# An H3 long convolution and an MLP on one core: unit (1,0)'s spectra without sums, last rows of y kept on chip, later matrix splits, and Strassen's scheme for one more block

## The chip, the cores and the metric

The kernel runs on one core of one Trainium2 chip. The time is the device time of one execution in microseconds. Before the change three timed runs took 859.74, 860.5 and 862.29 us, with a median of 860.5 us. The engines are TensorE (PE, with its weight loads shown as PEld), VectorE (DVE), ScalarE (ACT), GpSimd (POOL) and SyncE (SP); here SP issues nearly all DMA transfers. Each engine takes its instructions in the order in which the program gives them.

## The reference

Sequence length S is 2048, width D is 640, the MLP's inner width is 1728, all in float32. Cut to what matters:

```
x = A_q
for layer in range(2):
    x = x + A(layernorm(x), k, v, shift_k, ssm_k, ssm_D)
    x = x + relu(layernorm(x) @ w1) @ w2

def A(q, k, v, shift_k, ssm_k, ssm_D):
    kv = causal_conv4(k, shift_k) * v          # per channel
    y  = causal_conv_2048(kv, ssm_k)           # per channel, by FFT of length 4096
    return q * (y + kv * ssm_D)
```

`y` doesn't depend on `x`, so both layers use the same `y`, which the kernel computes once.

## The kernel before

The sequence is cut into 8 chunks of 256 rows (each two half chunks `s` of 128 rows), the width into 5 tiles of 128 channels.

*The convolution.* The work is done in units: one chunk and two channel tiles, or two chunks and one tile, or a single tile. Unit (c,t) is named by its first chunk and tile. `transform` computes for a unit the 256-point spectra of its `kv` (tile `at`) and of its piece of the filter (tile `gt`), both on TensorE with float32 matrices of cosines and sines (`cM`, `cG`, `cX`). For the filter, two sources `hf` and `hr` (the filter's chunk and the reversed chunk before it) are first added and subtracted on VectorE (`gs`, L415); TensorE multiplies these with four matrices, one bank per parity (`pg`, L470); ScalarE copies the odd bank (`ob`, L474), and VectorE forms sum and difference (`gt`, L475 and L476). For chunk 0, where only `hf` exists, the program multiplies `hf` directly with matrices and their negatives (L447), two banks, and ScalarE copies the banks to `gt` (L450). `products` multiplies spectra of chunk pairs on VectorE (768 columns in three parts, L592 to L596), adds them up, transforms back on TensorE (`pq`, L618 or L327 to L329) and writes the two half chunks of `y` to a tile `ys` (L650 and L651), which is stored to DRAM (L659). The spectra of chunks 0 to 5 also go out to DRAM (L540, L541) and are loaded again for later chunks. From the seventh unit on, the forward transform of `kv` uses `cM` as a pair of high and low parts (`csplit`, L319 to L323, whose results are `cMh` and `cMl`); later units use such a pair of `cG` as well.

*The weights.* `norms` loads `w1` and `w2` in 28 tiles (`ws`, L691), sums their squares on TensorE (`pw`, L698; the diagonal is taken by `dg`, L703; summed over partitions with a matrix of ones, `pn`, L705) and makes a power of two of each norm (`wsc`, L709). `wsplit` then splits each tile into a high and a low float16 part, on ScalarE (L725) and VectorE (L726), in an order in which the tiles of `w2` follow those of `w1` by WLAG = 3 groups.

*The MLP.* `main` runs once per block: (chunk, layer, half chunks). The first two chunks are done in halves, 8 short blocks; the other six chunks in whole blocks, 12 of them, in the order (2,0), (3,0), (2,1), (3,1), (4,0), (5,0), (4,1), (5,1), (6,0), (7,0), (6,1), (7,1), where the second number is the layer. A block goes through 7 groups `j` of 256 inner columns in the order JS = 0, 1, 2, 3, 6, 4, 5: the first product (`h`, L1024 to L1027, three passes of float16), the relu split into two float16 parts (`hh`, `hl`), and the second product (`o` and `oc`, L996 to L999), which runs one group behind. For a block in the list WINO the second product is done by Strassen's scheme with 7 products in place of 8 (L951), in six PSUM banks. It needs sums of `w2`'s quarters, which `wcombine` computes: DMA of `w2` again, four VectorE operations (`wc`, L755 to L758), a scaled copy on ScalarE (L766) and its low part on VectorE (`wt`, L767), one group after the other, and only after the last convolution product has written `gate`. Some groups of such a block stay plain, in the Strassen banks: group 6 always, and for a block of layer 0 before chunk 7 the first EARLY groups of JS too. `prep` forms a block's input: it loads `y` from DRAM (L842), takes the layer norm, multiplies by `y` (L845), adds, and normalizes again.

*The order of the work.* Nothing runs in the order of the program's text. Each operation is put into a list with its engine, a cost, what it reads and writes and a priority; `Plan.order` goes through time by these costs and gives each engine, when it is free, the ready operation of the best priority. The names are CRIT = -1, URGENT = 0, SOON = 1, CONV = 2, LATER = 2.5 and FILL = 3 (the MLP's matmuls are FILL), with the place in the program as the tie-break. It models DMA as one stream of a given bandwidth (DBW0 and DBW), and a buffer of a ring (`T(pool, tag, count, ...)`) must be free before an operation that first writes it can start. What comes out is the order on each engine's queue; on the chip an engine waits where its next instruction isn't ready. The loads of a unit have the unit's priority, and the weights' have SOON.

## Time and profile before

| | |
|---|---|
| median of three timed runs | 860.5 us |
| the profiled execution | 861.58 us |
| its span, first to last instruction | 859.8 us |
| PE, PEld busy | 842.6, 661.3 us |
| DVE, ACT, POOL busy | 743.3, 481.9, 46.5 us |
| mean granted clock of TensorE | 0.996 |
| DMA moved | 178.04 MB, mean 207 GB/s |

The profile shows one execution on the chip. A row of the order in time gives the start in us, the length in us, the engine, the source line, the operation, output and inputs by the program's tile names, their shape and type and a count of merged instructions; in square brackets stands the idle time of the engine before the row and what ended it. A row of the costliest groups gives the count, then busy us and mean ns, then idle us. Rows of DMA issues give the size and the median time from issue to landing. Matmuls are pipelined and their ends are modelled, so the starts of consecutive ones give their rate. "SPq" is SP's queue issuing a transfer.

### The profile page before, as it was taken

To read this page: it belongs to the slowest core of one execution; us is meant where nothing else is said; L and a number is where in the kernel's file an instruction comes from. 1 tells how busy PE (TensorE), PEld (TensorE's weight loads), DVE (VectorE), ACT (ScalarE), POOL (GpSimd) and SP (SyncE) were. 2 spreads that over 40 slices of the span, in tenths; PEclk is the share of its full clock that TensorE was granted. 3 is DMA by queue.
4 is the path that set the end of the run, shared out by engine and by line. 5 is a ranking of instruction groups with operands and counts; after the bars stand their busy time and mean duration, and the time that the engine had idled before them with its cause. 6 is when DMAs were issued, how large, how long until landed. Compare 5 with 4: busy or idle time off the path is not lost.

```text
span 859.8 us, 19550 instructions
## 1 busy us (share of the span) xinstructions
PE 842.6 (98%) x7738; PEld 661.3 (77%) x7738; DVE 743.3 (86%) x1367; ACT 481.9 (56%) x1121; POOL 46.5 (5%) x57
## 2 busy tenths in 40 slices
PE   8899999999999999999999999999999999999997
PEld 7777878777878777777777777778777777888886
DVE  6999999999889999999999998999897576645543
ACT  6597486455686375728448383745416275727331
POOL 2000000000011001101010000000000000000000
PEclk9999999999999999999999999999999999999999
DMA  9994868798999979889698879687985371110200
GB/s 325 389 295 136 261 197 295 213 344 280 312 249 294 315 205 260 214 247 249 199 245 245 225 230 167 177 192 237 260 285 200 109 240 32 41 23 1 42 21 32
DMA packets 133837, 178.04 MB, mean 207 GB/s; under 512 B 50545, under 2 KB 87153, under 8 KB 133746
## 3 DMA queue, kind: packets, MB, share of 16 engines
q1 hardware_dynamic: 125426, 166.31, 61.9%
q0 software_dynamic: 8320, 10.49, 8.3%
q8 instruction: 60, 0.98, 0.5%
q14 instruction: 31, 0.25, 0.1%
HBM read 122.03 MB, written 34.08 MB: 182 GB/s over the span
## 4 chain that ended last, share of the span: by engine, by line
PE 76%; DVE 14%; DMA 5%; ACT 2%; issue 2%; SPq 1%; DVEq 0%; ACTq 0%
PE h L1024 11%; PE h L1027 11%; PE h L1025 11%; PE o L997 7%; PE o L996 7%; PE o L999 7%; PE o L951 7%; DMA ws<-in_w 3%; DVE pd L595 3%; DVE pacc L596 3%; PE oc L996 2%; PE oc L997 2%; PE oc L999 2%; PE pq L618 1%; PE hb L1024 1%
## 5 line engine op out<-in xcount | busy, mean ns | idle before, releaser
L1027 PE MATMUL h<-xT,w 128*128 128x256 f16 (+1 forms) x1290 | 301.6, 252 | 0.4 <-DVE w L726 0.4
L1024 PE MATMUL h<-xT,w 128*128 128x256 f16 (+1 forms) x1290 | 301.9, 252 | 0.0
L1025 PE MATMUL h<-xT,w 128*128 128x256 f16 (+1 forms) x1290 | 301.7, 252 | 0.0
L1024 PEld LDWEIGHTS <-w 128*128 128x128 f16 x1390 | 136.1, 98 | 10.6 <-ACT w L731 0.4
L1025 PEld LDWEIGHTS <-w 128*128 128x128 f16 x1390 | 136.2, 98 | 10.3
L997 PE MATMUL o<-w,hh 128*128 128x512 f16 x364 | 137.9, 379 | 0.4 <-DVE w L726 0.4
L996 PE MATMUL o<-w,hh 128*128 128x512 f16 x364 | 138.1, 380 | 0.0
L1027 PEld LDWEIGHTS <-w 128*128 128x128 f16 x1290 | 126.4, 98 | 9.6 <-DVE w L726 0.6
L596 DVE TENSOR_TENSOR pacc<-pacc,pd 128x768 f32<-128x768 f32 x140 | 133.0, 951 | 0.5
L1080 ACT ACTIVATE hh<-h 128x512 f16<-128x512 f32 (+1 forms) x103 | 50.4, 489 | 102.1 <-PE h L1027 98.2
L997 PEld LDWEIGHTS <-hh 128*128 128x128 f16 x728 | 71.2, 98 | 45.7
L996 PEld LDWEIGHTS <-hh 128*128 128x128 f16 x728 | 71.2, 98 | 44.5 <-issue 0.2
L999 PE MATMUL o<-w,hl 128*128 128x512 f16 x234 | 88.7, 379 | 0.6 <-DVE hl L1081 0.6
L997 PE MATMUL oc<-w,hh 128*128 128x128 f16 x364 | 79.7, 219 | 0.0
L996 PE MATMUL oc<-w,hh 128*128 128x128 f16 x364 | 79.7, 219 | 0.0
L595 DVE TENSOR_TENSOR pd<-Ax,Gx 128x768 f32<-128x768 f32 x83 | 77.9, 951 | 0.7 <-DMA Gx<-G 0.5
L999 PEld LDWEIGHTS <-hl 128*128 128x128 f16 x468 | 45.8, 98 | 28.6 <-DVE hl L1081 1.1
L999 PE MATMUL oc<-w,hl 128*128 128x128 f16 x234 | 51.2, 219 | 0.0
L393 ACT ACTIVATE tp<-kt,shs 128x256 f32<-128x256 f32 (+1 forms) x78 | 42.7, 574 | 14.8 <-DVE acc L430 10.7
L1081 DVE SCALAR_TENSOR_TENSOR hl<-h,hh 128x512 f16<-128x512 f32 x55 | 37.7, 685 | 8.2 <-ACT hh L1080 8.2
L595 DVE TENSOR_TENSOR pd<-at,Gx 128x768 f32<-128x768 f32 x46 | 43.2, 952 | 1.7 <-DMA Gx<-G 1.6
L411 POOL DMA_DIRECT2D gs<-hr x20 | 19.6, 980 | 387.5 <-DVE pacc L592 189.5
(230 smaller groups left out, 1662.9 us busy)
## 6 DMA issues: line engine op xcount, KB each, us to landing
Ax<-A SPq DMA_DIRECT2D x89, 384.0 KB, 4.6
Gx<-G SPq DMA_DIRECT2D x89, 384.0 KB, 4.1
G<-gt SPq DMA_DIRECT2D x30, 384.0 KB, 4.9
A<-at SPq DMA_DIRECT2D x30, 384.0 KB, 4.4
y<-Y SPq DMA_DIRECT2D x30, 320.0 KB, 4.7
ws<-in_w SPq DMA_DIRECT2D x28, 320.0 KB, 6.6
x<-in_q SPq DMA_DIRECT2D x16, 320.0 KB, 4.6
out_dram<-x SPq DMA_DIRECT2D x16, 320.0 KB, 3.6
```

The costliest lines, as they stand in the source:

```text
L393: ACT.activation(o[:, i : i + m], kview(i, m, j), AF.Copy, scale=shs[:, t, j : j + 1])
L595: ew(f"mac{j % POOLMOD}", 768, lambda e, pd=pd, av=av, gv=gv: e.tensor_mul(pd.t, av(), gv()), [ax, gx], [pd], pr_)
L596: dve(768, lambda i=i, pd=pd: DVE.tensor_add(acc[:, i], acc[:, i], pd.t), [acc, pd], [acc], pr_)
L951: PE.matmul(b[:, c : c + w], x, y[:, z : z + w], start=done[i] == 1, stop=done[i] == total[i])
L996: PE.matmul(z, hh[:, c], wh[:, d], start=(j == JS[0] and i == 0 and (h == 0 or s == S[0])), stop=False)
L997: PE.matmul(z, hh[:, c], wl[:, d], start=False, stop=end and tail)
L999: PE.matmul(z, hl[:, c], wh[:, d], start=False, stop=end)
L1024: PE.matmul(p[:, z], wh, xv(t, 0), start=b, stop=False)
L1025: PE.matmul(p[:, z], wh, xv(t, 1), start=False, stop=tail and e)
L1027: PE.matmul(p[:, z], wl, xv(t, 0), start=False, stop=e)
L1080: act(2 * R, lambda p=p, hh=hh: ACT.activation(hh.t, p.t, AF.Relu), [p], [hh], URGENT)
L1081: dve(2 * R, lambda p=p, hh=hh, hl=hl: DVE.scalar_tensor_tensor(hl.t, p.t, 0.0, hh.t, op0=ALU.max, op1=ALU.subtract), [p, hh], [hl], URGENT)
```

## The change

1. `STRAIGHT` = ((1, 0),): unit (1,0)'s filter spectra are formed from `hf` and `hr` directly, as chunk 0's are from `hf`: 16 matmuls in place of 4, no `gs`, no `ob`, no `gt` sums on VectorE; ScalarE copies two banks. `cX` gets a third matrix (the negative of one of `cG`). Its `hf` and `hr` are loaded with priority SOON + 0.02, and the tiles of `w2` get SOON + 0.04, so these two loads stand between `w1` and `w2`.
2. `STRAIGHT_Y` = (1, 2, 4, 6): for these chunks, in layer 0, `prep` loads only those columns of `y` that were stored before the last unit of the chunk (a marker `YW` stands for their stores), and multiplies the last columns straight from that unit's `ys`, which stays in its buffer until then. All of `y` is still stored, for layer 1.
3. `ones` is a constant of its own and no longer takes one of the two `u` buffers.
4. The split of `cM` moves behind `wsplit` in the program, with the second split tile of `w2` group `JS[3]` as an added dependence.
5. `WINO` gets (6, 0), and `EARLY` is 2 and not 3. (6,0) is the only block to which EARLY applies: its groups 2, 3, 4 and 5 use Strassen's scheme, 0, 1 and 6 stay plain. All of the convolution and `wcombine` now stand in the program before the `prep` of (6,0) and not of (7,0).
6. The planner's `WLAG` is 4 and not 3, and its DMA model gets two stalls, 1.9 us at 3.5 and 1.3 us at 15.
7. `SIGNED` is a way to transform products back without the sum and difference on VectorE. It is empty, so none of its code runs; but its two matrices `cN` are loaded.

```diff
-WLAG = 3
+WLAG = 4
+STALLS = ((3.5, 1.9), (15.0, 1.3))
+SIGNED = ()
+CMJ = 3
+STRAIGHT_Y = (1, 2, 4, 6)
+STRAIGHT = ((1, 0),)
-WINO = ((7, 0), (6, 1), (7, 1))
-EARLY = 3
+WINO = ((6, 0), (7, 0), (6, 1), (7, 1))
+EARLY = 2
...
+                while best.nbytes and stalls and now >= stalls[0][0]:
+                    dma = max(dma, now + DLAT) + stalls.pop(0)[1]
...
+        straight = u[0] in STRAIGHT
...
-            dma(4 * n * wd, lambda x=x, src=src: SP.dma_start(x.t, pieces(u, src)), [], [x], LP.get(u[0], pr_))
+            dma(4 * n * wd, lambda x=x, src=src: SP.dma_start(x.t, pieces(u, src)), [], [x], SOON + 0.02 if straight and k[0] == "h" else LP.get(u[0], pr_))
...
-            if c0:
+            if c0 or straight:
                 gs.append((hf, lambda: hv(hf)))
                 continue
...
-        if c0:
+        if c0 or straight:
+            srcs = [hf] if c0 else [hf, hr]
             for b in range(2):
                 for ri in range(2):
+                    for k, x in enumerate(srcs):
...
+                        def f(b=b, ri=ri, k=k, x=x):
+                            for eo in range(2):
+                                neg = (b and eo) ^ (ri and k)
+                                m = cXt[:, ri if eo else 2, :] if neg else cGt[:, 2 * eo + ri, :]
+                                PE.matmul(e4(pg[b])[:, :, ri, :], m, hv(x)[:, eo], start=ri + eo + k == 0, stop=ri + eo + k == 1 + len(srcs))
...
+                        pe(8 * mm4, f, [x, cGt] + [cXt] * (b or ri and k), [pg[b]], pr_)
                 act(w, lambda b=b: ACT.activation(gt[:, :, 0:2, b, :], e4(pg[b]), AF.Copy), [pg[b]], [gt], pr_)
...
+                    early_w = c_ in STRAIGHT_Y and u[-1][1] < NDT - 1
...
+            for a in {c_ for c_, _ in u if u[-1][1] == NDT - 1 and c_ in STRAIGHT_Y}:
+                LASTY[a] = (ys, [t for c_, t in u if c_ == a][0], [i for i, (c_, _) in enumerate(u) if c_ == a])
...
-        ones = T(cv, "u", 2, [P, P], "ones", stream=1)
+        ones = keep(const, [P, P], "ones")
...
-                    dma(4 * D, lambda t=t, src=src: SP.dma_start(t.t, src), [], [t], SOON)
+                    dma(4 * D, lambda t=t, src=src: SP.dma_start(t.t, src), [], [t], SOON + 0.04 * k)
...
+            near = LASTY.pop(a, None) if layer == 0 else None
+            cut = near[1] * P if near else D
...
-                dma(4 * D, lambda s=s: SP.dma_start(ys[s].t, Y_d[s][a].t), [Y_d[s][a]], [ys[s]], SOON)
+                dma(4 * cut, lambda s=s: SP.dma_start(ys[s][:, 0:cut], Y_d[s][a].t[:, 0:cut]), [YW[a, s] if near else Y_d[s][a]], [ys[s]], SOON)
...
+                ew("ay", cut, lambda e, s=s, xn=xns[s]: e.tensor_mul(xn[:, 0:cut], ys[s][:, 0:cut], xn[:, 0:cut]), [ys[s], xns[s]], [xns[s]], URGENT)
+                if near:
+                    yt, k = near[0], near[2]
+                    ew("ay", D - cut, lambda e, s=s, xn=xns[s], yt=yt, k=k: e.tensor_mul(xn[:, cut:D], yt[:, s, k[0] : k[-1] + 1, :].rearrange("p a b -> p (a b)"), xn[:, cut:D]), [yt, xns[s]], [xns[s]], URGENT)
...
-    cXt = cload(cG[:, 4:6], "X", 2, CP[1], T(cv, "ru", NRU, [P, 2, P], "cX", stream=1))
+    cXt = cload(cG[:, 4:7], "X", 3, CP[1], T(cv, "ru", NRU, [P, 3, P], "cX", stream=1))
     cMt = cload(cM, "M", 6, CP[2])
+    cNt = cload(cG[:, 7:9], "N", 2, CP[2], T(cv, "ru", NRU, [P, 2, P], "cN", stream=1))
...
-    cMs = csplit(cMt, 6)
     conv_to(0)
...
     wsplit()
     xT = xTs[0]
+    cMs = csplit(cMt, 6, False, [WT[JS[CMJ], 1, 1]])
```

More of the change, by code (lines that the diff above doesn't have):

```diff
@@ L157, in when @@
             return max([now, *(when(d, depth - 1) for d in o.deps)]) + o.cost + 0.08
-        finish, later = [], []
+        finish, later, stalls = [], [], list(STALLS)
         now = 0.0
@@ L600, in products @@
         direct = u[-1][0] == 0
+        signed = direct and u[0] in SIGNED
         us = []
@@ L613, in products, with g @@
             fv = lambda f=f: f.r("p a (b c) -> p a b c", b=2)
+            if signed:
+                for s in range(2):
+                    def g(ri=ri, s=s, fv=fv):
+                        for kk in range(2):
+                            m = cNt[:, kk, :] if ri and not s else cMt[:, ri + 4 * kk, :]
+                            PE.matmul(pq[:, s * 256 : s * 256 + h], m, fv()[:, :, kk, :], start=ri + s + kk == 0, stop=ri + s + kk == 3)
+                    pe(8 * mm4, g, [f, cMt] + [cNt] * (ri and not s), [pq], pr_ if ri <= s or not s else BACK)
+                continue
             if full:
@@ L646, in products @@
             yo = lambda s: ys[:, s]
-        qs = T(cv, "qs", 1, [P, n, P], "qs" + nm)
-        act(h, lambda: ACT.activation(qs.t, pq[:, 256 : 256 + h].rearrange("p (a b) -> p a b", a=n), AF.Copy), [pq], [qs], pr_)
+        yq = lambda s: pq[:, s * 256 : s * 256 + h].rearrange("p (a b) -> p a b", a=n)
+        if signed:
+            for s in range(2):
+                act(h, lambda s=s: ACT.activation(yo(s), yq(s), AF.Copy), [pq], [dst[s]], (SOON, URGENT)[s])
+        qs = T(cv, "qs", 1, [P, n, P], "qs" + nm) if not signed else None
+        if not signed:
+            act(h, lambda: ACT.activation(qs.t, pq[:, 256 : 256 + h].rearrange("p (a b) -> p a b", a=n), AF.Copy), [pq], [qs], pr_)
         pp = lambda: pq[:, 0:h].rearrange("p (a b) -> p a b", a=n)
-        dve(h, lambda: DVE.tensor_sub(yo(0), pp(), qs.t), [pq, qs], [dst[0]], pr_)
-        dve(h, lambda: DVE.tensor_add(yo(1), pp(), qs.t), [pq, qs], [dst[1]] + [gate] * (u is units[-1]), BACK if direct else pr_)
+        if not signed:
+            dve(h, lambda: DVE.tensor_sub(yo(0), pp(), qs.t), [pq, qs], [dst[0]], pr_)
+            dve(h, lambda: DVE.tensor_add(yo(1), pp(), qs.t), [pq, qs], [dst[1]] + [gate] * (u is units[-1]), BACK if direct else pr_)
         if direct:
```

17 lines of the change are left out of this document (8 added, 9 removed).

## The prediction

> **What bounds the kernel now.** I read the page first: the busy shares, the 40 slices, the chain.
>
> ```profile
> span 859.8 us, 19550 instructions
> PE 842.6 (98%) x7738; PEld 661.3 (77%) x7738; DVE 743.3 (86%) x1367; ACT 481.9 (56%) x1121; POOL 46.5 (5%) x57
> ...
> DVE  6999999999889999999999998999897576645543
> ...
> PE 76%; DVE 14%; DMA 5%; ACT 2%; issue 2%; SPq 1%; DVEq 0%; ACTq 0%
> ```
>
> TensorE has matmuls in flight for 842.6 of 859.8 us, so at most 17.2 us are waits; the rest moves only if matmul work goes away or runs at a higher clock. VectorE is nearly as full until slice 30 (645 us) and has room after it. The profiled execution took 861.58 us (span 859.8, 1.8 around it); the three timed runs have median 860.5, 1.1 less. So I look for where TensorE waits. First TensorE's instructions in order of time, before the first MLP matmul (`h`), and the table of stretches (length, then busy us of PE, PEld, DVE, ACT, POOL, the granted clock, DMA share, GB/s):
>
> ```profile
> 40.81 0.71 PE L898 MATMUL xt<-ident,xh 128*128 128x128 f16 x5 [0.62 <-ACT xh L862]
> 42.33 0.72 PE L898 MATMUL xt<-ident,xl 128*128 128x128 f16 x5 [0.80 <-DVE wpw L708]
> 42.84 0.31 PE L1012 MATMUL h<-xT,w 128*128 128x128 f16 x1
> ```
> ```profile
> 35.65:42.84 7.19, 3.92 (x38) 2.70 (x39) 5.81 (x25) 5.77 (x11) 0.00 (x0) 0.82 1.06 385
> 42.84:46.90 4.06, 4.06 (x41) 4.06 (x40) 3.67 (x10) 3.39 (x8) 0.00 (x0) 0.50 1.03 403
> 48.00:60.00 12.00, 11.09 (x133) 8.67 (x131) 11.74 (x21) 11.63 (x26) 0.00 (x0) 1.00 0.98 294
> 60.00:80.00 20.00, 19.19 (x224) 14.09 (x222) 19.83 (x42) 15.21 (x29) 0.00 (x0) 1.00 0.39 130
> ```
>
> The MLP starts at 42.84. In the 7.19 us before it TensorE is idle 3.27 us, and the first 4.06 us of the MLP run at clock 0.50, which is 2.0 us lost. From 48 to 80 us 1.7 us more are lost. All later waits of TensorE that the timeline marks with over 0.5 us are these, 2.7 us in sum:
>
> ```profile
> 169.32 0.39 PE L999 MATMUL o<-w,hh 128*128 128x512 f16 x1 [0.59 <-DVE hh L1081]
> ...
> 176.13 1.18 PE L470 MATMUL pg<-gs,cG 128*128 128x256 f32 x4 [1.48 <-ACT at L520]
> ...
> 543.38 0.39 PE L999 MATMUL o<-w,hl 128*128 128x512 f16 x1 [0.59 <-DVE hl L1081]
> ```
>
> **The change part by part.** What holds the MLP start is VectorE's queue; its rows, with the DMA queue's issues:
>
> ```profile
> 14.90 0.17 DVE L779 TENSOR_SCALAR negmA<-sumq 128x2 f32<-128x2 f32 x1 [1.39 <-ACT jq L815]
> ...
> 22.51 0.95 DVE L322 TENSOR_TENSOR cMl<-cM,cMh 128x768 fp32r<-128x768 f32 x1
> ...
> 39.46 0.29 DVE L703 SCALAR_TENSOR_TENSOR dg<-pw,ident 128x128 f32<-128x128 f32 x1 [1.38 <-PE pw L698]
> 39.67 0.16 DVE L861 RECIPROCAL rstdB<-stdB 128x1 f32<-128x1 f32 x1
> ...
> 41.39 0.88 DVE L863 SCALAR_TENSOR_TENSOR xl<-xc,rstdB,xh 128x640 f16<-128x640 f32 x1
> ...
> 49.41 0.68 DVE L415 TENSOR_TENSOR gs<-hf,hr 128x512 f32<-128x512 f32 x1
> ...
> 73.58 0.68 DVE L475 TENSOR_TENSOR gt<-pg,ob 128x512 f32<-128x512 f32 x1
> ```
> ```profile
> 13.16 19.68 SPq L691 DMA_DIRECT2D ws<-in_w  x24
> ...
> 36.51 0.37 SPq L379 DMA_DIRECT2D hf<-in_hF  x1
> 37.27 0.37 SPq L379 DMA_DIRECT2D hr<-in_hR  x1
> ```
> ```profile
> ws<-in_w SPq DMA_DIRECT2D x28, 320.0 KB, 6.6
> ```
>
> Start of the MLP. The matrices' split (`cMl`) leaves a VectorE queue that is full from 15 to 37 us: -0.9 us (its 0.95 row less the overlap with the next); it comes back after the weight split, beside matmuls, at nothing on the path while VectorE has room, else 0.9. The second norm (`dg`), which waits for the last weight tile, stands ahead of `rstdB`; without it `rstdB` would run about 0.8 us earlier (39.67 less 39.46 is its own length, the wait was 1.38, and a square root stands before it). The new order is computed with two DMA stalls (1.9 and 1.3 us) that the old one did not know, so its idea of the last weight tile moves back and `rstdB`, `xh`, `xl` should be put ahead of `dg`: -0.8. Against it stand bytes. `cX` grows by 64 KB, a new `cN` of 128 KB, which nothing reads, goes out behind `cM` and ahead of `x`, on which VectorE already waits 1.39 us at 14.90: 192 KB at 385 GB/s is up to 0.5 us, I take +0.3. The `hf` and `hr` of unit (1,0), 512 KB, move from 36.5 to between `w1` and `w2`: another 1.4 us on the last `w2` tile. That is behind the first `h`, which needs only `w1` and `x`, unless `dg` still blocks the queue. `w1` and `w2` splits lie four groups apart instead of three, which gives `w2` a later due time, and no new instructions. Sum for the start: -1.4, from -1.7 to +1.9 (last weight tile 0.5 + 1.4 = 1.9 us later and `dg` still ahead).
>
> Spectra of (1,0) straight. TensorE's rows for a chunk-0 unit, which is computed this way already (two instructions are one fp32 matmul of 256 columns), and for (1,0) now:
>
> ```profile
> 16.04 0.59 PE L447 MATMUL pg<-hf,cG 128*128 128x256 f32 x2
> 16.47 0.59 PE L447 MATMUL pg<-hf,cX 128*128 128x256 f32 x2
> ...
> 52.36 1.08 PE L470 MATMUL pg<-gs,cG 128*128 128x256 f32 x4
> ```
>
> A matmul takes 0.43 us from start to start. Straight needs 2 halves x 2 parts x 2 sources x 2 parities = 16 of them, 6.9 us, in place of 4, 1.7 us. Off VectorE go two `gs` and two `gt` of about 0.6 us each, 2.4 us; ScalarE copies two banks instead of one. The weight tiles go out every 0.82 us from 13.16 on, four before; the h data follow the 14th (21.4 us) and land 6.6 us later, near 28 to 30 us, and the matmuls rank ahead of MLP matmuls (2 against 3), and the gap of 3.27 us before 42.84 shrinks with the earlier start, so I let 2.6 us of the 6.9 disappear in it and 4.3 us fall into the MLP: +2.6 net. Bounds: all hidden, -1.7; none hidden, +5.2.
>
> The clock. That filling makes the gap dense. Up to 40 us the clock holds while TensorE has such work, and the 0.50 comes after the thin 7.19 us; I take the nearest row, dense work before 35 us, and let the MLP start warm: -2.0 (bounds -2.0 and 0). The Trainium skill, "TensorE: Matmul & The Clock Gate", section "What's actually happening", has the gate fall to half after an idle window of about 3.4 us and rise after a busy one, with a free-running window. The 4.06 us at 0.50 agree with it; by that rule a gap filled only in part may still leave the start cold, and the sum would be 2.0 us higher.
>
> The MLP's first 40 us go at the pace of the weight split, which VectorE sets:
>
> ```profile
> L726 DVE SCALAR_TENSOR_TENSOR w<-ws,wsc,w 128x640 f16<-128x640 f32 x28 | 24.0, 878 | 0.6 <-ACT w L725 0.5
> ```
>
> 24.0 of its 33 us up to 73 us are this. It gets 0.8 (wait), 0.9 (`cMl`) and 1.2 (`gs`) us of room, so of the 1.7 us lost from 48 to 80 I let half go: -0.9 (bounds -1.7 and 0).
>
> `ones` among the constants frees a second `u` buffer in the start, where VectorE is full anyway: 0. Last rows of `y`:
>
> ```profile
> y<-Y SPq DMA_DIRECT2D x30, 320.0 KB, 4.7
> ```
>
> The last columns of chunks 1, 2, 4 and 6 are multiplied from SBUF, without store and reload (4.7 us for the reload). No wait of TensorE above names `y`, so I cost it at 0: what hides it is the MLP block in progress; without that cover each of the four is worth 4.7 us. It adds 8 short VectorE instructions, at most 0.41 each (the 256-wide row below), and holds a `u` buffer until the multiply; behind that the next product's `u` and its `pq` wait. Bounds: the two waits at 169 and 176 gone, -2.1, or as much added.
>
> Strassen for (6,0). The order in time (a common group of second products from its first row to the next `h`) and the chain (a Strassen group of 24 matmuls, and one common group cut for Strassen's banks, 30):
>
> ```profile
> 688.45 0.38 PE L996 MATMUL o<-w,hh 128*128 128x512 f16 x1
> ...
> 691.71 0.27 PE L1024 MATMUL h<-xT,w 128*128 128x256 f16 x1
> ```
> ```profile
> 745.77 2.86 PE o L951 x24
> ...
> 757.60 2.74 PE o L951 x30
> ```
>
> 3.26 against 2.86 us: 0.40 per group, and with EARLY 2 four of seven groups (2, 3, 4, 5) are Strassen's: -1.6. The cut group is 2.74 where five sixths of 3.26 are 2.72, so three cost +0.1. Sum -1.5, if the combined weights are there. They need the whole convolution to be done (`ys`, the gate); VectorE's rows of the gate and of groups 2 and 3, and when TensorE wants them now:
>
> ```profile
> 679.58 0.41 DVE L651 TENSOR_TENSOR ys<-pq,qs 128x256 f32<-128x256 f32 x1
> ...
> 700.43 1.55 DVE L767 SCALAR_TENSOR_TENSOR wt<-wc,wsc,wt 128x1280 f16<-128x1280 f32 x1 [1.09 <-ACT wt L766]
> ...
> 707.96 1.55 DVE L767 SCALAR_TENSOR_TENSOR wt<-wc,wsc,wt 128x1280 f16<-128x1280 f32 x1 [0.48 <-ACT wt L766]
> ```
> ```profile
> 701.52 0.38 PE L996 MATMUL o<-w,hh 128*128 128x512 f16 x1
> ...
> 707.50 0.38 PE L996 MATMUL o<-w,hh 128*128 128x512 f16 x1
> ```
>
> Group 2 would be ready at 702.0 for 701.5, group 3 at 709.5 for 707.5: late by 0.5 and 2.0 us as things stand, with VectorE's slices there at 5 to 7 tenths. The combination has no other client in (6,0), and VectorE's 2.4 us less work in (1,0) pull the gate forward, so I cost the lateness at 0; without that it is +2.0, plus what TensorE arrives earlier.
>
> Sum: -1.4 +2.6 -2.0 -0.9 -1.5 = -3.2: 858.4 for the profiled execution, 857.3 against the median.
>
> **The rivals.** (A) Slower: `dg` stays ahead of `rstdB` in VectorE's queue and the last weight tile lands 1.9 us later. The MLP starts at 44.7, the gap stays thin and cold, the straight spectra fall into the MLP: +1.9 +5.2 -1.5 = +5.6, 866.1. For it: the queue does exactly this now (39.46). Against: the order is computed anew with later weights. It decides once the first `h` starts after 43.
>
> (B) No change: the start is gained, but the gate is not, and at (6,0) TensorE waits for groups 2 and 3: 2.0 us as now plus the 1.7 gained before (-1.4 +2.6 -2.0 -0.9), which eats the sum: -3.2 +3.7 = +0.5, 861.0. For it: the rows above. Against: VectorE's free tenths.
>
> (C) The clock stays at half through the MLP's first 4 us: -3.2 +2.0 = -1.2, 859.3. For it: a gap filled only in part. It is the case of which the Trainium skill's page "TensorE: Matmul & The Clock Gate", cited above, speaks.
>
> (D) More: the waits at 169 and 176 go too, since VectorE has 2.4 us less to do before them: -3.2 -2.1 = -5.3, 855.2. Against: one of them hangs on where a transfer happens to stand in the queue.
>
> **How the numbers follow.** Within 0.3% is 857.9 to 863.1 around 860.5, about what a measurement can tell from no change. My forecast has 0.36 (855.8 to 858.8, of which 0.30 lies under 857.9), D or better 0.22, C 0.10, B 0.12, A 0.13, and 0.07 for other waits on the slow side. Faster: 0.30 + 0.22 + 0.03 (C's low end) = 0.55; same 0.06 + 0.07 + 0.12 = 0.25; slower 0.20. The time is the likeliest case, 857.3, its own range 855.8 to 858.8; the range over the cases goes from 852.5, which is D with 2.7 us more of the straight matmuls hidden, to 863.5, which leaves A out.
>
> **What would show it.** First `h` at 41.4 instead of 42.84, with `rstdB` ahead of `dg`; clock 1.00 in the MLP's first 4 us; `pg` from `hf` and `hr` before it; no `gs` and `gt` on VectorE for (1,0); four Strassen groups of 2.86 us in (6,0) with no gap in front of them; the two waits at 169 and 176 as they are or elsewhere. I am wrong if the straight matmuls stand in the MLP, if `dg` blocks, if `cN` delays `x`, or if TensorE waits for combined weights near 700.

## The result and the profile after

| | before | after |
|---|---|---|
| median, the kernels timed in turn on one chip | 860.88 us (859.74 to 862.29) | 853.49 us (852.80 to 853.89) |
| profiled execution (span) | 861.58 (859.8) | 853.36 (851.6) |

The ratio is 0.9918, with a 95% interval of 0.9905 to 0.9931: 7.4 us faster. The forecast was 857.3 us, with a range of 852.5 to 863.5. Against the profiled execution it was -3.2 us, and -8.2 came. The page of the kernel after: the span, the busy times, VectorE's 40 slices, the chain that ended last.

```profile
span 851.6 us, 19706 instructions
...
PE 841.1 (99%) x7796; PEld 666.9 (78%) x7796; DVE 749.1 (88%) x1401; ACT 486.6 (57%) x1131; POOL 46.0 (5%) x57
...
DVE  7999999999989999999999999999898587655643
...
PE 87%; DVE 4%; ACT 1%; issue 1%; DMA 0%; DVEq 0%
```

TensorE has 58 matmuls more, and is without one in flight for 10.5 us (851.6 - 841.1), where it was 17.2 before. The chain now runs through TensorE for 87% and not 76%; VectorE's share fell from 14% to 4%. So 6.7 of the 8.2 us are time without a matmul in flight that went. Where it went is read from one matmul that stands in each of the 20 blocks, the first down-projection (`hb` from `tb` and `down`). It is a milestone: its start before, less its start after, is what has been gained up to there. First before, then after, in the order of time on TensorE:

```profile
90.02 0.22 PE L1093 MATMUL hb<-tb,down 128*128 128x128 f16 x1
...
186.24 0.22 PE L1093 MATMUL hb<-tb,down 128*128 128x128 f16 x1
...
662.89 0.27 PE L1093 MATMUL hb<-tb,down 128*128 128x256 f16 x1
...
836.79 0.27 PE L1093 MATMUL hb<-tb,down 128*128 128x256 f16 x1
```
```profile
87.18 0.22 PE L1136 MATMUL hb<-tb,down 128*128 128x128 f16 x1
...
180.62 0.22 PE L1136 MATMUL hb<-tb,down 128*128 128x128 f16 x1
...
656.41 0.27 PE L1136 MATMUL hb<-tb,down 128*128 128x256 f16 x1
...
828.63 0.27 PE L1136 MATMUL hb<-tb,down 128*128 128x256 f16 x1
```

The gain is 2.8 us at the second block, 5.6 at the fifth, 6.5 at the sixteenth (the last before (6,0)) and 8.2 at the last. So 2.8 us come from the start, 2.8 from 90 to 186 us, 0.9 from there to 663 and 1.7 from (6,0) and what follows. Of TensorE's waits that the prediction listed (169, 176 and 543 us) none is left: from 60 to 830 us the view of waits shows no wait of TensorE. Between the second, the fifth and the sixteenth milestone both kernels do the same matmuls but for four transposes, so the milestones can be compared; the waits marked there add up to 2.1 and 0.8 us before and to almost nothing after.

The start after, on TensorE, on VectorE, and as a table of stretches with the columns of the prediction's table:

```profile
33.31 1.08 PE L459 MATMUL pg<-hf,cG 128*128 128x256 f32 x4
...
44.21 0.59 PE L459 MATMUL pg<-hr,cG 128*128 128x256 f32 x2
44.64 0.22 PE L1055 MATMUL h<-xT,w 128*128 128x128 f16 x1
```
```profile
36.91 0.16 DVE L904 RECIPROCAL rstdB<-stdB 128x1 f32<-128x1 f32 x1
...
39.23 0.88 DVE L906 SCALAR_TENSOR_TENSOR xl<-xc,rstdB,xh 128x640 f16<-128x640 f32 x1
...
40.94 0.49 DVE L945 COPY xT<-xt 128x640 f16<-128x640 f16 x1
...
44.13 0.29 DVE L741 SCALAR_TENSOR_TENSOR dg<-pw,ident 128x128 f32<-128x128 f32 x1
...
76.41 0.95 DVE L329 TENSOR_TENSOR cMl<-cM,cMh 128x768 fp32r<-128x768 f32 x1
```
```profile
33.30:44.64 11.34, 11.34 (x105) 9.78 (x103) 10.73 (x33) 9.54 (x18) 0.00 (x0) 1.00 1.02 384
44.64:48.70 4.06, 4.06 (x73) 4.06 (x72) 3.52 (x11) 3.66 (x10) 0.00 (x0) 1.00 0.89 286
48.70:60.00 11.30, 10.89 (x157) 9.04 (x155) 10.65 (x21) 11.22 (x25) 0.00 (x0) 1.00 1.04 314
60.00:80.00 20.00, 19.85 (x193) 14.47 (x191) 19.93 (x39) 17.70 (x38) 0.00 (x0) 1.00 0.66 208
```

The input `xT` is there at 41.4 us (40.94 + 0.49), but the first `h` starts at 44.64, 1.8 us later than before: all 16 straight matmuls, 6.9 us, stand ahead of it (the `pg` rows are their first and last). In return TensorE has no gap from 33 us on, the clock stays at 1.00, and the MLP's first 4.06 us hold 73 matmuls in place of 41.

At the other end stand the gate, the third set of combined weights (group 2, the first that (6,0) uses), and TensorE's first matmul with it:

```profile
669.80 0.41 DVE L683 TENSOR_TENSOR ys<-pq,qs 128x256 f32<-128x256 f32 x1
...
693.30 1.55 DVE L805 SCALAR_TENSOR_TENSOR wt<-wc,wsc,wt 128x1280 f16<-128x1280 f32 x1 [0.56 <-ACT wt L804]
```
```profile
695.46 0.43 PE L994 MATMUL o<-wt,gs 128*128 128x320 f16 x2
```

The convolution ends 9.8 us earlier than before (679.58). Group 2 is ready at 694.85 (693.30 + 1.55) and first used at 695.46: no wait, but 0.6 us to spare. The experiments show what lies behind that margin.

### The profile page after: what moved, and what is told of

The parts are those of the page before. It is cut to its first block, busy times and chain, and to the rows that moved or that the text cites. A ratio compares the mean times of both kernels' runs of the same rounds, so it can differ in the third digit from the quotient of the medians.

```text
span 851.6 us, 19706 instructions
## 1 busy us (share of the span) xinstructions
PE 841.1 (99%) x7796; PEld 666.9 (78%) x7796; DVE 749.1 (88%) x1401; ACT 486.6 (57%) x1131; POOL 46.0 (5%) x57
## 4 chain that ended last, share of the span: by engine, by line
PE 87%; DVE 4%; ACT 1%; issue 1%; DMA 0%; DVEq 0%
PE h L1067 12%; PE h L1070 12%; PE h L1068 12%; PE o L994 9%; PE o L1040 8%; PE o L1039 8%; PE o L1042 7%; PE oc L1040 2%; PE oc L1039 2%; PE oc L1042 2%; PE pq L644 1%; PE pg L482 1%; PE hb L1067 1%; PE hb L1068 1%; PE pr L334 1%; PE pt L505 1%
## 5 line engine op out<-in xcount | busy, mean ns | idle before, releaser
L1068 PEld LDWEIGHTS <-w 128*128 128x128 f16 x1390 | 136.0, 98 | 10.5
L1040 PE MATMUL o<-w,hh 128*128 128x512 f16 x336 | 127.3, 379 | 0.4 <-DVE w L764 0.3
L1039 PE MATMUL o<-w,hh 128*128 128x512 f16 x336 | 127.5, 380 | 0.0
L1123 ACT ACTIVATE hh<-h 128x512 f16<-128x512 f32 (+1 forms) x99 | 48.1, 486 | 94.3 <-PE h L1070 94.1
L1040 PEld LDWEIGHTS <-hh 128*128 128x128 f16 x672 | 65.8, 98 | 41.8
L1039 PEld LDWEIGHTS <-hh 128*128 128x128 f16 x672 | 65.7, 98 | 40.9
L1042 PE MATMUL o<-w,hl 128*128 128x512 f16 x208 | 78.8, 379 | 0.0
L1040 PE MATMUL oc<-w,hh 128*128 128x128 f16 x336 | 73.6, 219 | 0.0
L1039 PE MATMUL oc<-w,hh 128*128 128x128 f16 x336 | 73.6, 219 | 0.0
L1042 PEld LDWEIGHTS <-hl 128*128 128x128 f16 x416 | 40.7, 98 | 24.6 <-DVE hl L1124 0.2
L1042 PE MATMUL oc<-w,hl 128*128 128x128 f16 x208 | 45.6, 219 | 0.0
L1124 DVE SCALAR_TENSOR_TENSOR hl<-h,hh 128x512 f16<-128x512 f32 x51 | 35.0, 687 | 10.7 <-ACT hh L1123 10.4
L994 PE MATMUL o<-w,hh 128*128 128x192 f16 (+2 forms) x294 | 39.8, 255 | 0.0
```

The source lines that it names most:

```text
L994: PE.matmul(b[:, c : c + w], x, y[:, z : z + w], start=done[i] == 1, stop=done[i] == total[i])
L1039: PE.matmul(z, hh[:, c], wh[:, d], start=(j == JS[0] and i == 0 and (h == 0 or s == S[0])), stop=False)
L1040: PE.matmul(z, hh[:, c], wl[:, d], start=False, stop=end and tail)
L1042: PE.matmul(z, hl[:, c], wh[:, d], start=False, stop=end)
L1068: PE.matmul(p[:, z], wh, xv(t, 1), start=False, stop=tail and e)
L1123: act(2 * R, lambda p=p, hh=hh: ACT.activation(hh.t, p.t, AF.Relu), [p], [hh], URGENT)
```

## The experiments

All ran beside the kernel before on the same chip, whose median there was 860.64 to 860.70 us. The kernel after was timed in the first comparison only, beside a kernel before of 860.88 us. A variant's edit changes the list of operations, so the planner orders everything anew, and what a variant takes away is then not the edit alone. There are two exceptions, as the traces show instruction by instruction: the filled gap below, and the pairs that differ in Strassen's scheme for (6,0) alone, whose order is the same on every engine up to that block (some 680 us). Such pairs also show how much two executions of one order differ: the first `h` comes up to 2.1 us apart.

### One part out of the kernel after

Without the straight spectra:

```diff
-STRAIGHT = ((1, 0),)
+STRAIGHT = ()
```

> The changed kernel with STRAIGHT empty: unit (1,0)'s spectra are formed with the sums on VectorE again, everything else stays changed. Theory (filled gap): the changed kernel gains in the first 80 us because 6.9 us of spectra matmuls stand where TensorE idled (38 to 45 us) and keep its clock at 1.00 when the MLP starts. Without them the MLP's first matmul comes near 41.4 us, its first 4 us run at clock 0.50 (2.0 us), 1.7 us of pg matmuls fall into the MLP again and VectorE has 2.4 us more: 856 to 858 us, the marker of the first block's last group (55.83 us in the changed kernel) 2 us or more later than that less the earlier start. Rival (better order): the new DMA stalls in the order's model, the later w2 splits and the earlier start give the early gain; then this kernel stays at 854.5 us or less.

Measured 872.16 us (871.66 to 872.34), ratio to the kernel before 1.0128 (1.0104 to 1.0153): 18.7 us slower than the kernel after, and slower than before. Both theories missed.

Without the two stalls in the planner's DMA model, which puts nothing else on the chip than another order:

```diff
-STALLS = ((3.5, 1.9), (15.0, 1.3))
+STALLS = ()
```

> The changed kernel with STALLS empty: the order is computed with the old DMA model. Theory (filled gap): within 1 us of 853.5 us, since the spectra matmuls still stand before the first h. Rival (better order): dg stands ahead of rstdB again, as in the kernel before, the first h comes 1 us or more later than 44.64 us and the time is 855.5 us or more.

Measured 871.27 us (870.82 to 871.95), ratio 1.012 (1.0094 to 1.0145). The direction was the rival's, the size nobody's, and the rival's mark isn't there: `rstdB` (39.27) still stands ahead of `dg` (42.71), and the first `h` comes at 45.21, only 0.6 us later. In both runs one place holds the most of it. TensorE's order in time without the straight spectra, and VectorE's waits from 560 to 700 us (us in total, times, longest), there and in the kernel after:

```profile
714.42 0.42 PE L994 MATMUL o<-wt,gs 128*128 128x320 f16 x1 [8.76 <-ACT wt L804]
716.00 0.42 PE L994 MATMUL o<-wt,gs 128*128 128x320 f16 x1 [1.16 <-DVE wt L805]
```
```profile
DVE pd L609 <- DMA Gx<-G: 11.2, 6, 2.8
```
```profile
DVE pd L609 <- DMA Gx<-G: 1.2, 2, 0.8
```

TensorE stands still for 9.9 us in block (6,0) and waits for the third set of combined weights. Without the stalls it is 9.16 and 1.16. The convolution ended late (last `ys` at 685.34 and 685.14, after: 669.80), in part because VectorE's products waited 11.2 us for reloaded spectra of the filter (`Gx`; 7.3 us without the stalls). This is rival B's mechanism, with a price of 10 us and not 3.7.

Without the last rows of `y` taken from SBUF:

```diff
-STRAIGHT_Y = (1, 2, 4, 6)
+STRAIGHT_Y = ()
```

> The changed kernel with STRAIGHT_Y empty: all of y goes through DRAM again. Theory: no wait of TensorE hung on y, so 853.5 us within 0.7 us. Rival: keeping the last rows on chip is what removed TensorE's waits at 169 and 176 us (2.1 us) and near 543 us (0.6 us) and let the gate come at 670 and not 680 us; then they are back and the time is 855.5 us or more.

Measured 858.07 us (856.87 to 860.53), ratio 0.9964 (0.995 to 0.9979): 4.6 us slower than the kernel after, the rival's side. TensorE's waits from 60 to 660 us in this run (us in total, times, longest); the kernel after has none there:

```profile
PE h L1067 <- DVE hl L1129: 1.4, 1, 1.4
PE hb L1067 <- DVE hh L1124: 0.9, 1, 0.9
PE pg L482 <- ACT at L532: 0.9, 1, 0.9
PE o L1042 <- DVE hh L1124: 0.8, 1, 0.8
```

None of them names `y`. Three are late epilogues (`hh`, `hl`) and one a late copy of spectra on ScalarE (`at`), 4.0 us together. The milestones of this run stand at 86.81, 183.60, 412.14 and 661.85 us: 0.4 us ahead of the kernel after at the second block, 5.4 us behind it at the sixteenth.

Where the two part can be read, since VectorE's order is the same in both up to 128 us. The kernel after has its first columns of `y` then and multiplies by them; this run goes on with products, multiplies 5.2 us later, and forms the block's input `xh` 5.0 us later (146.91 for 141.94). First the kernel after, then this run:

```profile
128.78 0.69 DVE L885 TENSOR_TENSOR xnA<-y,xnA 128x512 f32<-128x512 f32 x1
```
```profile
133.94 0.81 DVE L885 TENSOR_TENSOR xnA<-y,xnA 128x640 f32<-128x640 f32 x1
```

Without Strassen's scheme for (6,0):

```diff
-WINO = ((6, 0), (7, 0), (6, 1), (7, 1))
+WINO = ((7, 0), (6, 1), (7, 1))
```

> The changed kernel without (6,0) in WINO. Theory: four groups cost 0.40 us more each and three cut groups 0.02 less: +1.5 us, 855.0 us, and no other change before 650 us beyond 0.5 us, since the order up to there hardly depends on it. Rival: part of the late gain comes from the convolution's end being pulled forward for (6,0); then more than 2 us go.

Measured 855.95 us (854.96 to 856.82), ratio 0.9948 (0.993 to 0.9966). By the medians the scheme is worth 2.5 us, on the rival's side, but the traces bear out the theory. The order is the same in both up to block (6,0), so no part of the gain comes from an order that (6,0) changed ahead of it. This execution began late (first `h` at 46.74, 2.1 us later), and 1.9 us of that stand at the sixteenth milestone (658.35) and at the last `ys` (671.74) too. From the sixteenth milestone to the last it takes 173.7 us, the kernel after 172.2: the scheme is worth 1.5 us.

### One part alone on the kernel before

Strassen for (6,0) alone:

```diff
-WINO = ((7, 0), (6, 1), (7, 1))
-EARLY = 3
+WINO = ((6, 0), (7, 0), (6, 1), (7, 1))
+EARLY = 2
```

> The kernel before with only (6,0) in WINO and EARLY 2. The prediction's rows had the combined weights of groups 2 and 3 late by 0.5 and 2.0 us as things stood. Theory: the gate comes early enough once the combination has a client in (6,0), since VectorE has free tenths there: -1.5 us, 859.4 us. Rival: TensorE waits 2 us for the weights near 700 us and the time is 860.5 us or more.

Measured 860.74 us (858.81 to 863.0), ratio 1.0005 (0.9992 to 1.0017): no change in the median. TensorE doesn't wait for combined weights (third set ready at 701.19, used at 702.74). From the sixteenth milestone to the last it is busy for 172.6 us, 1.3 less than in the kernel before, but 0.9 us of that goes into waits for epilogues (`tb` and `hl`, at 706 and 707 us) that the kernel before doesn't have there.

The straight spectra alone (the kernel after with every other part put back):

```diff
-WLAG = 4
+WLAG = 3
-STALLS = ((3.5, 1.9), (15.0, 1.3))
+STALLS = ()
-STRAIGHT_Y = (1, 2, 4, 6)
+STRAIGHT_Y = ()
-WINO = ((6, 0), (7, 0), (6, 1), (7, 1))
-EARLY = 2
+WINO = ((7, 0), (6, 1), (7, 1))
+EARLY = 3
...
-        ones = keep(const, [P, P], "ones")
+        ones = T(cv, "u", 2, [P, P], "ones", stream=1)
...
-    cNt = cload(cG[:, 7:9], "N", 2, CP[2], T(cv, "ru", NRU, [P, 2, P], "cN", stream=1))
+    cNt = None
...
+    cMs = csplit(cMt, 6)
...
-    cMs = csplit(cMt, 6, False, [WT[JS[CMJ], 1, 1]])
```

> The kernel before with only the straight spectra of (1,0) (and the order of loads that goes with them): no STALLS, WLAG 3, early split of cM, y through DRAM, ones in the u ring, (6,0) plain, no cN. Theory (filled gap): most of the early gain, 3 to 4.5 us, is there: 856.5 to 858 us, with the MLP starting at clock 1.00 and the spectra matmuls before it. Rival (better order): less than 1.5 us, 859.5 us or more.

Measured 861.81 us (859.82 to 862.93), ratio 1.0018 (1.0007 to 1.0028): a little slower, although the granted clock is 1.00 in the MLP's first 4.06 us here too (44.59 to 48.65). The two parts on which most of the forecast rested bring nothing by themselves.

### The start by itself

The kernel before with 48 matmuls more, which add zero to a sum while the last 8 weight tiles arrive. They carry no priority of their own, so the order on every engine stays that of the kernel before:

```diff
+NFILL = 8
...
+                        if k == 1 and 2 * JS.index(m // 2) + m % 2 >= 14 - NFILL:
+                            for _ in range(6):
+                                PE.matmul(pw2[:, 0], ident16.t, tb[:, 0:P], start=False, stop=False)
```

> The kernel before, in exactly its own order on every engine, with 48 float16 matmuls that add zero put ahead of the sums of squares of the last 8 w2 tiles, where TensorE waits for DMA between 34 and 39.5 us. Nothing else is changed. Theory: the clock is a term of its own: the MLP's first 4 us run at 1.00 and the time falls by up to 2.0 us, to 858.9 us, unless the weight split, which sets the pace to 73 us, takes part of it back as waits of TensorE. Rival: the split takes all of it: 860.5 to 861.5 us, with the clock at 1.00 and longer waits between 48 and 80 us. Second rival: the gap from 39.5 to 42.3 us, still unfilled, lets the clock fall anyway.

Measured 863.79 us (861.01 to 868.32), ratio 1.004 (1.0019 to 1.0061): slower. The stretches before and after its first `h` (42.16 us), and two milestones of this run; the row from 216.76 us is that of the kernel before:

```profile
35.65:42.16 6.51, 4.44 (x66) 3.94 (x64) 5.88 (x25) 5.46 (x11) 0.00 (x0) 0.92 1.06 378
42.16:46.22 4.06, 4.06 (x55) 4.06 (x54) 3.75 (x10) 3.92 (x9) 0.00 (x0) 0.71 1.04 412
```
```profile
88.50 0.22 PE L1097 MATMUL hb<-tb,down 128*128 128x128 f16 x1
...
216.78 0.22 PE L1097 MATMUL hb<-tb,down 128*128 128x128 f16 x1
```
```profile
216.76 0.22 PE L1093 MATMUL hb<-tb,down 128*128 128x128 f16 x1
```

The clock fell in what was left of the gap, as the second rival had it: it stands at 0.50 from 41.10 to 44.51 us, which makes a mean of 0.71, and the MLP leads by 1.5 us at 88 us (88.50 for 90.02). That the filling did this is not shown. The run with Strassen's scheme for (6,0) alone has the same order up to 680 us without any filling, and in its execution the MLP's first 4.06 us have a mean of 0.70, and the lead is 1.8 us (88.21):

```profile
41.81:45.87 4.06, 4.06 (x54) 4.06 (x53) 3.61 (x10) 3.99 (x8) 0.00 (x0) 0.70 1.03 412
```
```profile
661.20 0.27 PE L1093 MATMUL hb<-tb,down 128*128 128x256 f16 x1
```

That lead lasts: at 661.20 it is still 1.7 us (662.89 before). In the filled run it is gone at 217 us, and the end is 2 us later than before. VectorE had the lead as well (its rows stand 1.5 us earlier at 90 us, 1.4 at 140) and lost it by 176 us, where it waits for loads: 0.9 us for `y` and 2.1 for `Gx`, against none and 1.6 in the kernel before. So a lead of this size lasted to block (6,0) in one execution of this order and not in another. From 413 us on the filled run loses more, 0.7 us of it in a wait of TensorE at 460 us for a copy on ScalarE (`ob`); the rest was not found.

The kernel after with the straight matmuls ranked behind the MLP's:

```diff
-                        pe(8 * mm4, f, [x, cGt] + [cXt] * (b or ri and k), [pg[b]], pr_)
+                        pe(8 * mm4, f, [x, cGt] + [cXt] * (b or ri and k), [pg[b]], FILL + 0.5 if straight else pr_)
```

> The changed kernel with the priority of the straight spectra's matmuls put behind the MLP's (3.5 in place of 2): they run before the first h only where TensorE has nothing else. The first h, which waits behind 3.6 us of them at 41.0 to 44.64 us, can then start near 41.5 us. Theory: the first 30 us of the MLP go at the weight split's pace, so starting h earlier moves the markers by less than 1 us: 853 to 854 us. Rival: TensorE bounds this stretch, and the earlier start gives 2 us or more: 851.5 us or less.

Measured 858.4 us (856.96 to 859.64), ratio 0.9972 (0.996 to 0.9984). The first `h` came at 43.13, 1.5 us earlier than in the kernel after, and the end 4.9 us later. Its stretches from the first `h` on:

```profile
43.13:47.19 4.06, 4.06 (x76) 4.06 (x74) 3.68 (x7) 3.51 (x9) 0.00 (x0) 1.00 1.04 393
47.19:60.00 12.81, 9.34 (x111) 7.53 (x109) 12.03 (x27) 11.30 (x25) 0.00 (x0) 0.84 1.10 271
```

From 47 to 60 us TensorE is idle for 3.5 us (its waits name the split weights `w` with 1.7 us, the epilogues `tb` and `hh` with 1.8) and the mean clock falls to 0.84. The MLP that starts earlier runs into the work of VectorE and ScalarE; in these two plans the straight matmuls do less harm ahead of it than behind.

### Is it the parts or the plan?

Two edits that leave the change as good as whole. The first drops a load that nothing reads (it also leaves free the buffer of a ring in which it lay); the second makes the split of `cM` at the start again:

```diff
-    cNt = cload(cG[:, 7:9], "N", 2, CP[2], T(cv, "ru", NRU, [P, 2, P], "cN", stream=1))
+    cNt = None
```

> The kernel after, without the load of cN (128 KB that nothing reads, ahead of x on the DMA queue). Theory by bytes: 128 KB at 385 GB/s are 0.34 us of DMA before the weight tiles: 853.2 us, from 852.6 to 853.7. Rival: any change of the list of operations shifts the whole order of the planner, and the time moves by more than 1.5 us either way.

```diff
+    cMs = csplit(cMt, 6)
...
-    cMs = csplit(cMt, 6, False, [WT[JS[CMJ], 1, 1]])
```

> The kernel after, with the split of the matrix cM made at the start again, ahead of the convolution's first unit. Theory: VectorE gets 0.95 us of cMl back among its full stretch from 15 to 37 us, which was priced at 0.9 us on the path: 853.5 + 0.9 = 854.4 us (853.5 to 855.2). Rival 1: the straight matmuls fill TensorE up to the first h at 44.6 us, so the later xl is covered: 853.5 us within 0.5. Rival 2: the order is planned anew and the convolution ends later ahead of block (6,0), by which the time moves by more than 2 us.

Measured 872.1 us (870.57 to 874.41), ratio 1.014 (1.0119 to 1.016), and 870.8 us (870.3 to 872.43), ratio 1.0125 (1.011 to 1.0141). With 128 KB less to load the kernel is 18.6 us slower. Both rivals that spoke of the plan were right, and the place is the same again. VectorE's gate and third set with the early split, TensorE's first use of that set, and the stretches around the wait without the dead load:

```profile
684.21 0.42 DVE L683 TENSOR_TENSOR ys<-pq,qs 128x256 f32<-128x256 f32 x1
...
713.27 1.55 DVE L805 SCALAR_TENSOR_TENSOR wt<-wc,wsc,wt 128x1280 f16<-128x1280 f32 x1 [0.32 <-ACT wt L804]
```
```profile
713.29 0.42 PE L994 MATMUL o<-wt,gs 128*128 128x320 f16 x1 [8.76 <-ACT wt L804]
```
```profile
700.00:713.00 13.00, 4.42 (x40) 3.54 (x38) 9.61 (x22) 8.15 (x20) 0.00 (x0) 0.83 0.53 156
713.00:719.00 6.00, 4.50 (x21) 2.76 (x21) 5.12 (x8) 3.81 (x7) 0.00 (x0) 0.51 0.52 136
```

The wait is paid twice: behind it the mean clock is 0.51 for some 6 us.

Last, two of the four late runs once more with (6,0) plain, which takes the wait for combined weights out of that block:

```diff
-STRAIGHT = ((1, 0),)
-WINO = ((6, 0), (7, 0), (6, 1), (7, 1))
+STRAIGHT = ()
+WINO = ((7, 0), (6, 1), (7, 1))
```

> The kernel after, with the spectra of unit (1,0) in the two-stage form again, and with block (6,0) out of the Strassen list. With (6,0) in the list, the run without straight spectra took 872.16 us, 18.7 more than the kernel after, with a wait of 10 us (8.76 and 1.16) of TensorE for the first combined weights in block (6,0). Theory: that wait is a consequence of the late end of the convolution (last ys 31 us ahead of the middle of block (6,0) in the kernel after, 20 us in that run) and goes with the Strassen form of (6,0), while some 7 us lost at 0 to 210 us stay: about 872.2 - 9.9 + 1.5 (the Strassen form's worth) = 863.8 us (862.5 to 865), and the straight spectra are still worth some 8 us beside the 855.95 us of the run with (6,0) plain alone. Rival: the late end of the convolution itself comes from the plan with the four-block list; then without (6,0) in the list the straight spectra are worth at most 3 us: 859 us or less.

```diff
-STALLS = ((3.5, 1.9), (15.0, 1.3))
+STALLS = ()
...
-WINO = ((6, 0), (7, 0), (6, 1), (7, 1))
+WINO = ((7, 0), (6, 1), (7, 1))
```

> The kernel after, without the two DMA stalls in the planner's costs, and with block (6,0) out of the Strassen list. With (6,0) in the list the run without the stalls took 871.27 us with a wait of 10.3 us (9.16 and 1.16) for combined weights in block (6,0). Theory: the wait goes with the Strassen form of (6,0) and the rest stays: about 871.3 - 10.3 + 1.5 = 862.5 us (861 to 864). Rival: the planner's stalls matter only by the end of the convolution; then this run is within 1.5 us of the 855.95 us of the run with (6,0) plain alone.

Measured 860.34 us (859.24 to 861.56), ratio 0.9999 (0.9989 to 1.0008), and 859.61 us (857.58 to 863.26), ratio 0.9996 (0.9982 to 1.0009). Both lie between theory and rival. The convolution still ends late (last `ys` at 683.60 and 684.60), so its lateness doesn't come from the longer list, which was the rival's reason; but the wait was worth more than the 8.4 and 8.8 us that I took for it. The slow clock was left out: in the two runs with the wait TensorE is busy for 5.25 and 5.12 us at 0.50 behind it, an estimated 2.6 us lost in each. As a table of medians:

| | (6,0) by Strassen's scheme | (6,0) plain |
|---|---|---|
| kernel after | 853.49 | 855.95 |
| without straight spectra | 872.16 | 860.34 |
| without the planner's stalls | 871.27 | 859.61 |
| kernel before (with EARLY 2; as it was) | 860.74 | 860.70 |

In each row both kernels have the same order up to (6,0), so a row compares that block, within the scatter of the start. The same scheme for the same block brings 2.5 us (1.5 by the milestones), brings nothing, or costs 11.8 and 11.7 us. Beside a plain (6,0), where no wait for weights can hide the rest, the straight spectra with the plan that comes with them are worth 4.4 us and the stalls 3.7.

What decides is when the convolution ends. A row per kernel: VectorE's busy time from 40 to 640 us of the profiled execution, VectorE's waits for `Gx` from 560 to 700 us, its last `ys`, when the third set is ready, when TensorE uses it, and TensorE's wait for it.

| | VectorE busy | waits for `Gx` | last `ys` | third set ready | used | wait |
|---|---|---|---|---|---|---|
| kernel after | 584.9 | 1.2 | 669.8 | 694.9 | 695.5 | 0 |
| without last rows of `y` | 582.7 | 2.1 | 675.2 | 700.0 | 700.9 | 0 |
| straight matmuls last | 579.9 | 1.7 | 676.5 | 700.0 | 700.5 | 0 |
| before, Strassen for (6,0) | 581.8 | 0.7 | 677.9 | 701.2 | 702.7 | 0 |
| without stalls | 574.6 | 7.3 | 685.1 | 714.9 | 713.4 | 10.3 |
| without straight spectra | 575.8 | 11.2 | 685.3 | 716.0 | 714.4 | 9.9 |
| early split | 573.7 | 9.2 | 684.2 | 714.8 | 713.3 | 9.9 |
| without dead load | 571.1 | 7.7 | 688.3 | 714.9 | 713.3 | 9.8 |

The first column comes from stretches like these two, of the kernel after and of the one without the dead load:

```profile
40.00:640.00 600.00, 599.38 (x5660) 465.84 (x5658) 584.88 (x1006) 356.10 (x837) 41.95 (x40) 1.00 0.88 248
```
```profile
40.00:640.00 600.00, 596.16 (x5604) 462.65 (x5603) 571.14 (x985) 355.97 (x834) 42.08 (x40) 1.00 0.84 240
```

The convolution's work on VectorE is nearly the same in all of them, so up to 14 us more of idle VectorE go with a convolution that ends up to 18 us later. VectorE's longest wait in all four late runs is for reloaded spectra of the filter, 7.3 to 11.2 us against 0.7 to 2.1. Why these loads come late in those plans was not followed. Up to a last `ys` of 678 us the third set follows 23 to 25 us behind it and is in time. At 684 us and later it follows 27 to 31 us behind, since the combination then falls among the epilogues and norms of (6,0) and its neighbour on VectorE and ScalarE (from the last `ys` to the third set ScalarE is busy for 11.6 us in the kernel after and for 21.8 without the straight spectra): 6 us of lateness become 10 us of wait. (A wait is shorter than the set's readiness suggests, because TensorE starts with the high parts and waits 1.2 us more for the low ones.)

No run beat the kernel after. `wcombine` makes the sets in the order of the groups and so begins with two that (6,0), with EARLY 2, doesn't use. Beginning with group 2 would bring the first needed set forward by two of its steps (5.8 and 7.9 us apart in the kernel after); this wasn't tried.

## Why the prediction was right in sign and short in size

*Start of the MLP, -1.4, and straight spectra, +2.6.* As predicted, `rstdB` stands ahead of `dg`, and the input is ready at 41.4 us. The reason given, the two stalls, isn't needed for it: without them `rstdB` stands ahead of `dg` too (39.27 and 42.71). The step that failed is "I let 2.6 us of the 6.9 disappear in it and 4.3 us fall into the MLP". All 6.9 us stand ahead of the MLP, since their priority of 2 goes before the MLP's 3 for as long as one of them is ready. First `h` +1.8 us, four matmuls less later (-1.7): together +0.1, where the two terms gave +1.2. Rival A's mark ("once the first `h` starts after 43") was wrong with it: `h` came at 44.64 for another reason, without rival A's loss. Such sizes hold for these two executions: other executions of the two orders have the first `h` at 41.81 and 46.74, and the medians differ by 7.4 us where these two profiles differ by 8.2.

*The clock, -2.0.* Right: 1.00 in the MLP's first 4.06 us, as in the other runs with the straight matmuls ahead of the MLP. But 2.0 us is what the profiled execution of the kernel before lost; another execution of its order lost 1.2 (mean clock 0.70 and not 0.50). Whether a gap filled in part leaves a cold start, rival C's condition, the runs don't settle, since the filled and the unfilled gap came out alike (0.71 and 0.70).

*Waits from 48 to 80, -0.9.* Right in size: what is left of the 2.8 us at the second block, with +0.1 and -2.0 taken off, is -0.9. A second execution of each order agrees: from the first `h` to that milestone it takes 42.5 us twice after, and 47.2 and 46.4 before, the 0.8 between these being the clock. Whether such a lead lasts is another matter, as the two executions of the old order above show.

*Last rows of `y`, 0.* Wrong. The step was "no wait of TensorE above names `y`, so I cost it at 0". Taking this part away costs 4.6 us, nearly all between the second block and 412 us. What the part moves is a block's input: at the first place where the orders part, it comes 5.0 us earlier, near the 4.7 us that the prediction had for a reload without cover. With it the order of VectorE's work changes, and the waits that come back without the part name other tiles. How the 5.0 us there become 5.5 us of the MLP by 412 us was not followed further.

*The later waits, 0.* Wrong, and the largest miss: they went, 2.8 us from 90 to 186 and 0.9 to 663, -3.7 in all, of which the three listed waits are 2.7. Rival D had the mechanism, at -2.1, and only for the first two. The sum of the terms with the measured sizes is +0.1 -2.0 -0.9 -3.7 -1.7 = -8.2.

*Strassen for (6,0), -1.5, with the weights' lateness at 0.* Right: 1.7 by the milestones, 1.5 against the same order with (6,0) plain, and no wait. The reason given (less work on VectorE pulls the gate forward) is not borne out: with the straight spectra alone the last `ys` came at 680.34, no earlier than the 679.58 before. And the term stood on 0.6 us of margin, and 0 to +3.7 was too narrow a view of its risk: four of the plans near this one pay 10 us of wait and the slow clock behind it, and end at 871 to 872, some 8 us above the top of the range. That this plan met the deadline was in part luck as well.

*`ones`, 0.* Not tried by itself, and neither was WLAG.

What the prediction didn't see is that the parts don't add. It costed each edit on the order of the kernel before; alone two of them bring nothing, taken out singly five cost 2.5 to 18.7 us. Much of the 7.4 us belongs to the one plan that came out of all of them together, and that the time lies inside the range is in part luck: 853.49 is 1 us above its lower end, and in the profiles the terms missed by 5.0 us (-3.2 for -8.2), more than the 4.8 from the forecast to that end.

## What to carry to other kernels

Where a planner writes the order, an edit's price is that of a new plan: before crediting a part, find the one deadline that all plans share (here the end of the convolution against the first combined weights) and read its margin, because a few us on the wrong side may cost far more than the part brings. Follow milestones through the trace, not the place of the edit: a lead gained early can go again in waits for loads. And read a second execution of the same order before you price a start by one profile; here two of them put the first `h` up to 2.1 us apart. Last, put what a scheme needs first at the head of the queue that makes it: the combined weights are made in an order in which the first needed one is the third.

## What the runs showed of the hardware

The clock fell without any long pause. In the run without the straight spectra TensorE works from 36 to 42 us in pieces of 0.46 us with pauses of 0.35 to 0.66 us, and the clock is below full. TensorE's order in time, and the stretches:

```profile
37.02 0.46 PE L736 MATMUL pw<-ws 128*128 128x128 bf16 x5 [0.36 <-DMA ws<-in_w]
...
40.05 0.71 PE L941 MATMUL xt<-ident,xh 128*128 128x128 f16 x5 [0.66 <-ACT xh L905]
```
```profile
35.65:42.16 6.51, 4.41 (x45) 3.45 (x42) 5.66 (x16) 6.17 (x11) 0.00 (x0) 0.69 1.06 380
42.16:46.22 4.06, 4.06 (x49) 4.06 (x48) 2.48 (x7) 2.28 (x5) 0.00 (x0) 0.65 1.05 405
```

TensorE is busy for 68% of that first stretch, and the clock is 0.50 from 38.17 to 44.99 us. In the kernel before it was alike: no pause from 36 to 43 us is over 0.80 us. The Trainium skill, "TensorE: Matmul & The Clock Gate", section "A second HAM failure mode: psum-queue depth-cycling", tells of a kernel whose frequent short pauses made the clock swing; these rows agree, with DMA as the cause of most of the pauses. Its section "What's actually happening" has half clock follow an idle window of about 3.4 us; the 8.6 us of wait without the dead load, and the clock of 0.51 behind it, agree with that; the start of the kernel before, which the prediction read so, had no pause near that long.

Short pauses don't always do it. The same order with (6,0) plain has the like pauses (0.28 to 0.96 us) in its execution, is busy for less of the time (57%), and keeps a clock of 1.00; what decides was not found:

```profile
33.70:40.21 6.51, 3.72 (x48) 2.59 (x47) 5.95 (x21) 5.60 (x11) 0.00 (x0) 1.00 1.05 385
40.21:44.27 4.06, 4.06 (x75) 4.06 (x72) 4.06 (x13) 4.06 (x8) 0.00 (x0) 1.00 1.06 391
```

At any moment of these traces the granted clock is 1.0 or 0.5, and what lies between is a mean over the stretch. The stretches at 0.5 inside the program last 3.4 us (41.10 to 44.51 in the filled run) or about two, three or four times that (6.8 before, 10.2 without the dead load, 13.7 without the stalls).

A full TensorE hides a lot: in 600 us from 40 us on, the kernel after and the one without the dead load differ by 3.2 us on TensorE (599.4 and 596.2 busy) and by 13.7 us on VectorE. The second number went with the end of the convolution, and the page's shares of the whole span (99% for TensorE after) don't show it.
